# Where the sequence additions, the check's sums and the next norm stand in an adaLN, Fourier mixing and SwiGLU block

## The chip, the cores and the metric

The kernel runs on one core of one Trainium2 chip. The metric is the device time of one execution in microseconds (us); the time before is a median of 710.24 us. TensorE (PE) does the matrix products, VectorE (DVE) and ScalarE (ACT) work on tiles of 128 partitions, GpSimd (POOL) and SyncE (SP) mostly start transfers.

## The reference

`x` has 2048 rows of 512 columns. Six vectors of 512 come from `silu(c) @ w_mod`; they shift, scale and gate the two halves of the block.

```python
mod = (_silu(c) @ w_mod).reshape(c.shape[0], 6, 1, -1)
sa, ca, ga, sb, cb, gb = (mod[:, 0], ..., mod[:, 5])
h = _layernorm(x, axis=-1) * (1 + ca) + sa
# y = Real(DFT_seq(DFT_hidden(h))):  a = h @ Wd_re.T, b = h @ Wd_im.T,  y = Ws_re @ a - Ws_im @ b
x = x + ga * _A_ref(h, A_dft_seq_re, A_dft_seq_im, A_dft_hid_re, A_dft_hid_im)
h = _layernorm(x, axis=-1) * (1 + cb) + sb
# out = (silu(h @ w1) * (h @ w3)) @ w2, with 1792 inner columns
x = x + gb * _B_ref(h, B_w1, B_w3, B_w2)
```

## The kernel before, in words

Every fp32 product is made of three products of parts (`product`, L100): high by high, high by low, low by high. ACT makes a high part (a copy in the short format, L87), DVE the low part (the rest, L90). So each tile that PE is to multiply passes through ACT and then DVE.

The work has three stages. First come the first norm and the transform over the 512 columns, ordered by a small planner (`task`, `arrange`). Then comes the transform over the 2048 rows ("the sequence stage", `seq_unit`, L750): 32 units in two halves `j`, and while PE runs a unit, DVE prepares a later one (tiles `l`, `d`, `bh`). At last comes the feed-forward part. The output has four groups of 512 rows, `t` = 0 to 3, in two pairs `PAIRS = ((0, 2), (1, 3))`. Groups 0 and 2 are ready after the first half of the sequence stage, 1 and 3 after the second.

The order inside each engine is the order in which the Python code records instructions. Work that has no fixed place waits in a queue `background` of steps, each with an estimate of its DVE and ACT time. After each piece of PE work `advance` takes steps from the queue until the time of that piece is used up; a `PAUSE` ends one such turn. A second queue, `jobs`, holds the splitting of weights and goes first.

The names that the prediction uses:

- `mod_columns` makes one of four vectors (`ga`, `sb`, `cb1`, `gb`) on DVE: weights `wmc` times `silu(c)` (step `scale`, L96), then sums (step `total`, L356 and L362).
- `residual` (L805) adds a gated result to a group's rows `xr`. `add_sums` does it twice for a group, from a copy `sum` of accumulators; after the second half of the sequence stage four such steps, eight instructions, stand at the end of `background`.
- `ln2(t)` is the second norm of group `t` as some 25 steps: `a1` to `a3` the mean and the difference `xc`, `a3b` squares on ACT, `a4`, `rows` and `partition_sums` the sum of squares, `a6` the root on ACT (with a table load), `a6b` its inverse and spread over rows, `a7` the product (DVE, L96) and `a8` scale and shift (ACT, L894). Between them are `PAUSE`s. `chunk_parts` then splits `xc` into `h2h` (ACT) and `h2l` (DVE), the right-hand operand of `up`.
- `up(g, t)` runs four `up_block`s of 12 matmuls, `w1` then `w3` for two halves `q`. A `w1` block ends in a Silu on ACT (L1094), a `w3` block in a product `v` on DVE (L96), a high part `hf` on ACT and its low part on DVE. `up` uses PSUM banks 0 to 3 in turn.
- `down_unit` is six matmuls with `w2`; here it uses banks 4 to 7 in turn, and ACT empties each (`y`, L335). POOL starts the transfer that adds two of them to the result in memory (L1146).
- After `up(0, 0)` and `up(1, 0)` come eight `down` units of group 0, called D1 to D8 here, then `up(0, 2)`, which needs `h2h` and `h2l` of group 2. D5 takes the bank that D1 used.
- From then on 12 `items` run in seven "factor" units for `w1` (`a1` to `a7`) and seven for `w3` (`b1` to `b7`), with eight `down` units (`y`) between. `turning` is 5, the first item of pair 1. The last factors of an item run in the head of the next: `-b7 a1 a2 -b4 -b3`. `b4` adds to the bank that DVE must have read after `b7`.
- `judge` adds up sums of squares (`chk`) which tell whether the matrices have the symmetry that the kernel uses: a memset of `sq` on POOL (L1005) and 14 small DVE instructions (L1006 to L1026).

Of the kernel before, what the change touches and what calls it, by code (L numbers as in the profile page):

```python
# [8 lines left out]
F32 = mybir.dt.float32  # L9
# [3 lines left out]
OP = mybir.AluOpType  # L13
AX = mybir.AxisListType

P = 128
N = 512
# [5 lines left out]
ND = D // P  # L23
# [19 lines left out]
def folded(nc, pools, c, cp, wmr, wmc, x, xt, ctr, cti, wdr, wdi, w1, w3, w2, out):  # L43
# [8 lines left out]
    consts, small, big, psum, dram, tc = pools  # L52
# [6 lines left out]
    def take(dt=F32, what="s"):  # L59
        slot = free.popleft()  # L60
        count[0] += 1
        t = big.tile([P, 2, N], dt, name=f"{what}_{count[0]}", tag=f"slot{slot}")
        slot_of[id(t)] = (slot, t)
        return t

    def give(t):
        slot, _ = slot_of.pop(id(t))
        free.append(slot)

    def bank(i):  # L70
# [12 lines left out]
    def cols(i):  # L83
        return slice(i * P, (i + 1) * P)

    def copy(dst, src, scale=1.0):
        nc.scalar.activation(dst, src, AF.Copy, scale=scale)  # L87
# [7 lines left out]
    def times(dst, a, b):  # L95
        nc.vector.tensor_tensor(out=dst, in0=a, in1=b, op=OP.mult)  # L96

    def product(acc, lhs, rhs, first, last, more=False):
        for n, (a, b) in enumerate(PASSES):
            nc.tensor.matmul(  # L100
                acc,
                lhs[a],
                rhs[b],
                start=first and n == 0,
                stop=last and n == len(PASSES) - 1,
                skip_group_check=more,
            )


    background = deque()  # L110
# [3 lines left out]
    def step(queue, slots, fn, dve=0.0, act=0.0):  # L114
        queue.append((slots, dve, act, fn))
# [128 lines left out]
    for k in range(2, 4):  # L244
# [7 lines left out]
        out=ident,  # L252
        in_=ident,
# [9 lines left out]
        out=anti,  # L263
        in_=anti,
# [72 lines left out]
    sc_row = []  # L337
# [6 lines left out]
    def mod_columns(v, dst):  # L344
        w = {}

        def fetch(i):
            w[i] = take(F32, "wmc")
            nc.sync.dma_start(w[i], wmc[v, i])

        def scale(i):
            times(w[i], w[i], sc_row[0][:, 0, :].unsqueeze(1).to_broadcast([P, 2, N]))

        def total(i):
            r1 = small.tile([P, 32], F32, name=f"r1_{v}_{i}", tag="r1")
            nc.vector.tensor_reduce(  # L356
                out=r1,
                in_=flat(w[i]).rearrange("p (a b) -> p a b", b=32),
                axis=AX.X,
                op=OP.add,  # L360
            )
            nc.vector.tensor_reduce(  # L362
                out=dst[:, 2 * i : 2 * i + 2],
                in_=r1.rearrange("p (a b) -> p a b", b=16),
                axis=AX.X,
                op=OP.add,
            )
            give(w[i])

        def end():  # L370
            if dst is cb1:
                nc.vector.tensor_scalar(cb1, cb1, 1.0, None, op0=OP.add)
            if dst is ga:
                nc.vector.tensor_scalar(ga2, ga, -2.0, None, op0=OP.mult)
            if dst is gb:
                give(sc_row[0])
            done.add(("mod", v))

        for i in range(2):
            step(background, 1, lambda i=i: fetch(i))  # L380
        background.extend([PAUSE] * 2)
        for i in range(2):
            step(background, 0, lambda i=i: scale(i), 1.2)
            step(background, 0, lambda i=i: total(i), 1.3)
        step(background, 0, end, 0.1)


# [427 lines left out]
    xc, sums = {}, {}  # L815
# [187 lines left out]
    def judge():  # L1003
        sq = consts.tile([P, 3, 32], F32, name="sq")
        nc.gpsimd.memset(sq, 0.0)  # L1005
        nc.vector.tensor_reduce(  # L1006
            out=sq[:, 0, :8],
            in_=chk.rearrange("p a b n -> p (a b) n"),
            axis=AX.X,
            op=OP.add,  # L1010
        )
# [12 lines left out]
        times(fine[:, 0:2], fine[:, 0:2], fine[:, 2:4])  # L1024
        times(fine[:, 0:1], fine[:, 0:1], fine[:, 1:2])
        nc.vector.tensor_scalar(bad, fine[:, 0:1], -1.0, 1.0, op0=OP.mult, op1=OP.add)  # L1026
# [25 lines left out]
    def give_w(key):  # L1052
        for t in wuse.pop(key):
            give(t)

    hf = {}
    turn = [0, 0]
    cur = {}
# [4 lines left out]
    def behind(units, fn):  # L1063
        if units:
            later.setdefault(units, []).append(fn)
        else:
            fn()
# [5 lines left out]
            later[n - 1] = later.pop(n)  # L1073


    def up_block(g, t, q, w):
        if q == 0 and w == "w1":
            drain(lambda: ("h2", t, 1) in done)
        to = bank(turn[0] % 4)
        turn[0] += 1  # L1080
        for d in range(ND):
            at = slice(d * P, (d + 1) * P)
            product(
                to,
                [u[:, q, at] for u in wuse[w, g]],
                [u[t, d // 2][:, d % 2, :] for u in (h2h, h2l)],
                d == 0,
                d == ND - 1,
            )
        if t == PAIRS[0][1] and q == 1:  # L1090
            give_w((w, g))
        if w == "w1":
            cur["v"] = take(F32, "v")
            nc.scalar.activation(cur["v"][:, 0, :], to, AF.Silu)  # L1094
        else:
            v = cur.pop("v")
            times(v[:, 1, :], v[:, 0, :], to)
            u = hf[g, t, q] = take(F32R, "hf")
            copy(u[:, 0, :], v[:, 1, :])
            behind(1, lambda: minus(u[:, 1, :], v[:, 1, :], u[:, 0, :].bitcast(F32)))  # L1100
            behind(1, lambda: give(v))
# [395 lines left out]
    for m in range(2):  # L1497
        todo.popleft()
        name = f"seq{m}"
# [53 lines left out]
                w_low((w, 0))  # L1553
    give(zz)

    USED = {"w1": (0.0, 0.5), "w3": (1.2, 0.5), "y": (0.0, 0.6), "own": (0.7, 0.0)}
    FACTOR = {
# [6 lines left out]
    def beside(us, used):  # L1566
        advance(us - used[0], us - used[1], jobs)
        if not jobs:
            advance(0.0, 0.0)

    def up(g, t):
        for q in range(2):
            for w in ("w1", "w3"):
                drain(lambda: ((w, g), "l") in done, jobs)
                delayed()
                up_block(g, t, q, w)
                beside(2.72, USED[w])

    def down(g, pair, t, d, key):
        drain(lambda: (key, "l") in done, jobs)  # L1580
# [13 lines left out]
    for g in range(2):  # L1594
        for d in range(ND):
            down(g, 0, 0, d, ("w2", g))
    judge()
    up(0, 2)
    load_w(("w3", *items[0]))
    weight_jobs(0, "w1")  # L1600
# [8 lines left out]
    turning = len([at for at in items if at[1] == 0])  # L1609
# [45 lines left out]
        beside(1.36, FACTOR[kind][n])  # L1655

    weight_jobs(0, "w3")
    ln2(1)
    ln2(3)
    for i in range(len(items)):  # L1660
        body = "a6 a5 y a7 y y a4 y a3 y b1 y b2 y b6 b5 y"
        if i == turning:
            body = "y y y y y a6 y a5 y a7 y b1 b2 a4 b6 a3 b5"
        if i == len(items) - 1:
            body = "a6 a5 y a7 y y a4 y a3 b1 y b2 b6 b5 y b7 y b4 y b3 y y y y y y y y"
        head = "-b7 a1 -b4 -b3 a2 " if i == turning else "-b7 a1 a2 -b4 -b3 " if i else "a1 a2 "
# [813 lines left out]
```

## Time and profile before

| | |
|---|---|
| time, median of 3 runs | 710.24 us (709.85 to 710.78) |
| the profiled execution's own time | 708.46 us |
| its span in the profile | 706.7 us |
| mean granted PE clock | 0.991 |
| PE busy | 686.3 us, 97% |
| DVE busy | 548.3 us, 78% |
| ACT busy | 430.8 us, 61% |
| POOL busy | 119.4 us, 17% |

The profile is of one execution. Its times count from the start of the span. A timeline row reads: start, duration, engine, source line, operation, output tile, input tiles, shape, how many, and in brackets how long the engine stood idle before it and which instruction ended that.

### The profile page before, as it was taken

Reading aid. Unit: us, or ns where it says so; the run is one execution under the profiler, and the core shown is the slowest. Engines: PE = TensorE matmul, PEld = TensorE weight load, DVE = VectorE, ACT = ScalarE, POOL = GpSimd, SP = SyncE. Lnnn points to the kernel's source line nnn. Section 1 sums busy time; section 2 is a strip of 40 time slices with the busy share of each in tenths; the row PEclk is TensorE's granted clock in tenths of the full one; section 3 lists DMA queues with packets and bytes.
Section 4 is the critical chain, followed back from the end, with each engine's and each line's share of the span. In section 5 each row is a group of like instructions: output and inputs, shape, how many; then the busy total and the mean of one; then the engine's idle time right before and its main releaser. Section 6 shows DMA issues by size and latency. Waiting matters only on the chain.

```text
span 706.7 us, 8912 instructions
## 1 busy us (share of the span) xinstructions
PE 686.3 (97%) x3152; PEld 564.7 (80%) x3152; DVE 548.3 (78%) x877; ACT 430.8 (61%) x709; POOL 119.4 (17%) x141
## 2 busy tenths in 40 slices
PE   7999999999999999899999999999999999999995
PEld 4898888888888888687888788787788888888784
DVE  5999679997999978579987886896865556664763
ACT  4998865545454655745677676867665565656420
POOL 1320253542524000200100101011010100101000
PEclk9999999999999999999999999999999999999998
DMA  8730299796678521522868558376763847537403
GB/s 266 211 120 1 77 373 328 251 307 229 207 283 287 168 86 41 92 58 64 209 114 199 89 130 153 61 156 137 239 136 73 180 62 175 111 69 162 137 0 124
DMA packets 38100, 108.93 MB, mean 154 GB/s; under 512 B 4896, under 2 KB 5152, under 8 KB 38048
## 3 DMA queue, kind: packets, MB, share of 16 engines
q0 software_dynamic: 12352, 43.00, 29.3%
q1 hardware_dynamic: 25264, 63.98, 27.5%
q10 hardware_dynamic: 432, 1.31, 0.5%
q8 instruction: 26, 0.43, 0.3%
q14 instruction: 26, 0.21, 0.1%
HBM read 76.81 MB, written 33.55 MB: 156 GB/s over the span
## 4 chain that ended last, share of the span: by engine, by line
PE 81%; DVE 7%; ACT 6%; issue 2%; DMA 2%; SPq 1%; ACTq 0%; DVEq 0%
PE bank L100 52%; PE bank L750 25%; PE bank L559 2%; PE bank L598 1%; DMA wmr<-in_wmr 1%; ACT xc L894 1%; PE bank L576 1%; DVE xc L96 1%; SPq L231 1%; ACT hf L87 1%; ACT y L335 1%; DVE v L96 0%; DVE hl L90 0%; ACT hm L501 0%; DMA w<-in_wdi 0%
## 5 line engine op out<-in xcount | busy, mean ns | idle before, releaser
L100 PE MATMUL bank<-hf,w2h 128*128 128x512 f32 (+1 forms) x452 | 140.9, 391 | 0.3
L1146 POOL DMA_DIRECT2D sum<-y x48 | 41.0, 855 | 390.1 <-ACT y L335 373.0
L100 PEld LDWEIGHTS bank<-hf,w2h 128*128 128x128 f32 x452 | 84.3, 188 | 22.1 <-DVE hf L90 3.4
L100 PE MATMUL bank<-hf,w2l 128*128 128x512 f32 (+1 forms) x226 | 87.6, 388 | 0.0
L87 ACT ACTIVATE hf<-v 128x512 fp32r<-128x512 f32 x56 | 35.3, 630 | 67.3 <-DVE v L96 62.7
L335 ACT ACTIVATE y<-bank,gb 128x512 f32<-128x512 f32 x96 | 64.9, 682 | 18.6 <-PE bank L100 18.3
L93 DVE TENSOR_TENSOR v<-bank,x 128x512 f32<-128x512 f32 x36 | 24.7, 685 | 34.9 <-PE bank L100 34.8
L750 PE MATMUL bank<-bh,us 128*128 128x512 f32 x128 | 49.9, 390 | 0.0
L93 DVE TENSOR_TENSOR x<-bank,x 128x512 f32<-128x512 f32 x36 | 24.7, 687 | 32.4 <-PE bank L100 28.7
L750 PE MATMUL bank<-bh,ul 128*128 128x512 f32 x128 | 49.8, 389 | 0.0
L750 PE MATMUL bank<-d,us 128*128 128x512 f32 x128 | 49.8, 389 | 0.0
L750 PE MATMUL bank<-d,uh 128*128 128x512 f32 x128 | 49.8, 389 | 0.0
L750 PE MATMUL bank<-l,us 128*128 128x512 f32 x128 | 49.8, 389 | 0.0
L750 PE MATMUL bank<-l,uh 128*128 128x512 f32 x128 | 49.8, 389 | 0.0
L100 PEld LDWEIGHTS bank<-hf,w2l 128*128 128x128 f32 x226 | 42.4, 188 | 8.4
L90 DVE TENSOR_TENSOR hf<-v,hf 128x512 fp32r<-128x512 f32 x56 | 38.5, 687 | 12.2 <-ACT hf L87 12.1
L170 POOL DMA_INDIRECT re<-in_ctr,mirror x32 | 35.8, 1117 | 66.2 <-DVE ul L90 39.5
L1224 ACT ACTIVATE v<-v 128x512 f32<-128x512 f32 x36 | 22.8, 632 | 38.8 <-DVE v L93 38.8
L87 ACT ACTIVATE x<-bank 128x512 f32<-128x512 f32 x72 | 41.4, 586 | 7.2 <-PE bank L100 6.5
L170 POOL DMA_INDIRECT im<-in_cti,mirror x32 | 32.7, 1023 | 35.3 <-PE bank L750 10.0
L100 PE MATMUL bank<-h2h,w1h 128*128 128x512 f32 x80 | 31.8, 397 | 1.5 <-ACT h2h L87 1.5
L100 PE MATMUL bank<-h2l,w1h 128*128 128x512 f32 x80 | 31.9, 399 | 0.8 <-DVE h2l L90 0.8
(246 smaller groups left out, 1775.2 us busy)
## 6 DMA issues: line engine op xcount, KB each, us to landing
sum<-y POOLq DMA_DIRECT2D x48, 512.0 KB, 5.6
w<-in_w SPq DMA_DIRECT2D x42, 512.0 KB, 4.5
re<-in_ctr SPq DMA_DIRECT2D x32, 256.0 KB, 5.0
im<-in_cti SPq DMA_DIRECT2D x32, 256.0 KB, 5.0
wmc<-in_wmc SPq DMA_DIRECT2D x8, 512.0 KB, 6.3
xr<-in_xt SPq DMA_DIRECT2D x8, 512.0 KB, 7.6
sum<-xr SPq DMA_DIRECT2D x8, 512.0 KB, 6.2
x<-in_x SPq DMA_DIRECT2D x11, 256.0 KB, 4.8
```

The lines of the kernel that those rows point to most:

```text
L87: nc.scalar.activation(dst, src, AF.Copy, scale=scale)
L90: nc.vector.tensor_tensor(out=dst, in0=a, in1=b, op=OP.subtract)
L93: nc.vector.tensor_tensor(out=dst, in0=a, in1=b, op=OP.add)
L96: nc.vector.tensor_tensor(out=dst, in0=a, in1=b, op=OP.mult)
L100: nc.tensor.matmul(acc, lhs[a], rhs[b], start=first and n == 0, stop=last and n == len(PASSES) - 1, skip_group_check=more,)
L170: nc.gpsimd.indirect_dma_start(dst, None, rows, bass.IndirectOffsetOnAxis(ap=at, axis=0))
L231: queue.dma_start(raw_w[dt][q * 64 : (q + 1) * 64, m, :], w[i][par::2, q])
L335: nc.scalar.activation(dst, src, AF.Identity, scale=by)
L559: nc.tensor.matmul(halves(hb[k])[:, m, :], sides((hh, hl)[a][k])[:, dt, m, :], wu[dt][:, b, m, :], start=False, stop=dt % 2 == 1 and n == ...
L750: nc.tensor.matmul(acc[what, e], lhs, rhs, start=begin and i == 0, stop=(end or (turn and what == "x")) and i == len(terms) - 1, skip_grou ...
L1146: nc.gpsimd.dma_start(sums[t, d // 2], y, accum_op=OP.add)
L1224: behind(k != 0 or q == 0, lambda: nc.scalar.activation(v, src, AF.Silu))
```

## The change

It does five things. `mod_columns` uses, in place of one product over 1024 columns and one sum of it, eight multiply-and-sum instructions of 128 columns (with `accum_out`), and each step has an estimate of 0.9 us where two had 1.2 and 1.3. `fill_pauses`, called once after the sequence stage, takes the six last steps of `background` (the four `add_sums` and two releases of tiles) and puts each `add_sums` ahead of one of the last four pauses of `ln2(2)`. `up_block` is recorded in two halves, with a turn of `advance` after each. `ln2(1)` and `ln2(3)` enter the queue ahead of `up(0, 2)`. `judge` moves from there to the head of item 7.

```diff
-            step(background, 0, lambda i=i: scale(i), 1.2)
-            step(background, 0, lambda i=i: total(i), 1.3)
+            for b in range(2):
+                step(background, 0, lambda i=i, b=b: total(i, b), 0.9)
...
+        def total(i, b):
+            sums, junk = parts[i], w[i][:, b, :]
+            for n in range(ND):
+                nc.vector.scalar_tensor_tensor(
+                    junk[:, cols(n)], junk[:, cols(n)], 1.0, sc_row[0][:, 0, cols(n)],
+                    op0=OP.mult, op1=OP.mult, accum_out=sums[:, b, n : n + 1],
+                )
...
+    def fill_pauses():
+        last = [background.pop() for _ in range(6)][::-1]
+        fillers = [last[:1], last[1:3], last[3:4], last[4:]]
+        at = len(background)
+        while fillers:
+            at -= 1
+            if background[at][-1] is None:
+                for slots, _, _, fn in fillers.pop()[::-1]:
+                    background.insert(at, (slots, 0.0, 0.0, fn))
...
-                up_block(g, t, q, w)
-                beside(2.72, USED[w])
+                for part in range(2):
+                    up_block(g, t, q, w, part)
+                    beside(1.36, USED[w] if part else (0.0, 0.0))
...
-    judge()
+    ln2(1)
+    ln2(3)
     up(0, 2)
...
     weight_jobs(0, "w3")
-    ln2(1)
-    ln2(3)
     for i in range(len(items)):
+        if i == turning + 2:
+            judge()
```

In the listings below a row is line, operation, output, inputs and shape; numbers after a name count tiles.

ACT from the last high part of `up(1, 0)` through the first `down` units, before. `v_2714` is the last product of `up(1, 0)`, `y_2743` and `y_2769` empty the banks of D1 to D4, `xc_2564` and `xc_2611` are the two halves of group 2 in `a8`:

```order
L87 ACTIVATE hf_2737<-v_2714 128x512
L880 ACT_TABLE_LOAD
L880 ACTIVATE s_377_2721<-s_377_2721,eps 32x16
L335 ACTIVATE y_2743<-bank_382_2744,gb 128x512
L335 ACTIVATE y_2743<-bank_383_2759,gb 128x512
L335 ACTIVATE y_2769<-bank_385_2770,gb 128x512
L894 ACTIVATE xc_2564<-xc_2564,sb,cb_151 128x512 x2
L335 ACTIVATE y_2769<-bank_386_2780,gb 128x512
```

and now, from the root of `ln2(2)` on; `v_2781` is the last product, `hf_2805` its high part, `y_2812` empties D1 and D2, `xc_2546` and `xc_2616` are the halves of group 2:

```order
L883 ACT_TABLE_LOAD
L883 ACTIVATE s_364_2700<-s_364_2700,eps 32x16
L1101 ACT_TABLE_LOAD
L1101 ACTIVATE v_2734<-bank_368_2721 128x512
L87 ACTIVATE w2h_2736<-w_366_2716 128x1024
L87 ACTIVATE w2h_2747<-w_367_2718 128x1024
L87 ACTIVATE hf_2765<-v_2734 128x512
L1101 ACTIVATE v_2781<-bank_376_2768 128x512
L897 ACTIVATE xc_2546<-xc_2546,sb,cb_151 128x512 x2
L87 ACTIVATE hf_2805<-v_2781 128x512
L897 ACTIVATE xc_2616<-xc_2616,sb,cb_151 128x512 x2
L335 ACTIVATE y_2812<-bank_382_2813,gb 128x512
```

The root and its two table loads now stand ahead of the splitting of `w2`, and both halves of `a8` and the last `hf` ahead of the first `y`.

DVE over the same stretch, before: the last product of `up(1, 0)`, the inverse root, `a7` twice and the low parts of group 2.

```order
L96 TENSOR_TENSOR v_2714<-v_2714,bank_378_2723 128x512
L90 TENSOR_TENSOR hf_2737<-v_2714,hf_2737 128x512
L883 RECIPROCAL s_377_2721<-s_377_2721 32x16
L847 COPY w_382_2753<-s_377_2721 32x16 x4
L848 STREAM_TRANSPOSE stat_2556<-w_382_2753 128x512
L96 TENSOR_TENSOR xc_2564<-xc_2564,stat_2556 128x1024
L96 TENSOR_TENSOR xc_2611<-xc_2611,stat_2556 128x1024
L90 TENSOR_TENSOR h2l_2821<-xc_2564,h2h_2819 128x1024
```

and now:

```order
L90 TENSOR_TENSOR w2l_2749<-w_367_2718,w2h_2747 128x1024
L886 RECIPROCAL s_364_2700<-s_364_2700 32x16
L850 COPY w_374_2752<-s_364_2700 32x16 x4
L851 STREAM_TRANSPOSE stat_2538<-w_374_2752 128x512
L96 TENSOR_TENSOR v_2734<-v_2734,bank_372_2740 128x512
L90 TENSOR_TENSOR hf_2765<-v_2734,hf_2765 128x512
L96 TENSOR_TENSOR xc_2546<-xc_2546,stat_2538 128x1024
L808 SCALAR_TENSOR_TENSOR xr_2382<-sum_2605,ga,xr_2382 128x512 x2
L96 TENSOR_TENSOR xc_2616<-xc_2616,stat_2538 128x1024
L808 SCALAR_TENSOR_TENSOR xr_2106<-sum_2605,ga,xr_2106 128x512 x2
L96 TENSOR_TENSOR v_2781<-v_2781,bank_378_2786 128x512
L90 TENSOR_TENSOR hf_2805<-v_2781,hf_2805 128x512
```

The inverse, both `a7` and four of the eight additions (`xr`) now stand ahead of the last product `v_2781`, which stood ahead of them; the other four additions stand further up, two on either side of the second product of `up(0, 0)`.

POOL around the memset of `judge`, before, with the transfers that start after D4, D6 and D8 ahead of it:

```order
L1146 DMA sum_1_2265<-y_2769 128x1024
L1146 DMA sum_0_2263<-y_2790 128x1024
L1146 DMA sum_1_2265<-y_2810 128x1024
L1005 MEMSET sq 128x96
L1146 DMA sum_0_2631<-y_3074 128x1024
```

There it stood behind the last transfer of D1 to D8. POOL now:

```order
L1153 DMA sum_1_3155<-y_4704 128x1024
L1153 DMA sum_0_3591<-y_4746 128x1024
L1153 DMA sum_1_3593<-y_4794 128x1024
L1008 MEMSET sq 128x96
L1153 DMA sum_0_3153<-y_4934 128x1024
```

The memset stands behind the start of a `down` result's transfer in both; now that is the last `down` unit of item 6, directly ahead of `b7`. On DVE the 14 instructions stand between the last work for that `down` unit and the addition that reads the bank of `b7`.

More of the change, by code (lines that the diff above doesn't have):

```diff
@@ L349, in fetch @@
             nc.sync.dma_start(w[i], wmc[v, i])
[L351 to L368, printed above, removed]
+        def total(i, b):
+            sums, junk = parts[i], w[i][:, b, :]
+            for n in range(ND):
+                nc.vector.scalar_tensor_tensor(
+                    junk[:, cols(n)],
+                    junk[:, cols(n)],
+                    1.0,
+                    sc_row[0][:, 0, cols(n)],
+                    op0=OP.mult,
+                    op1=OP.mult,
+                    accum_out=sums[:, b, n : n + 1],
+                )
+            if b:
+                nc.vector.tensor_reduce(
+                    out=dst[:, 2 * i : 2 * i + 2], in_=sums, axis=AX.X, op=OP.add
+                )
+                give(w[i])
+        parts = [
+            small.tile([P, 2, ND], F32, name=f"r1_{v}_{i}", tag="r1") for i in range(2)
+        ]
         def end():
@@ L1073, in delayed, with up_block @@
             later[n - 1] = later.pop(n)
-    def up_block(g, t, q, w):
-        if q == 0 and w == "w1":
+    def up_block(g, t, q, w, part):
+        if q == 0 and w == "w1" and part == 0:
             drain(lambda: ("h2", t, 1) in done)
-        to = bank(turn[0] % 4)
-        turn[0] += 1
-        for d in range(ND):
+        if part == 0:
+            cur["to"] = bank(turn[0] % 4)
+            turn[0] += 1
+        to = cur["to"]
+        for d in range(2 * part, 2 * part + 2):
             at = slice(d * P, (d + 1) * P)
@@ L1089, in up_block @@
             )
+        if part == 0:
+            return
         if t == PAIRS[0][1] and q == 1:
@@ L1554, in folded @@
     give(zz)
+    def fill_pauses():
[7 more added lines that the diff above has]
+                    background.insert(at, (slots, 0.0, 0.0, fn))
+    fill_pauses()
     USED = {"w1": (0.0, 0.5), "w3": (1.2, 0.5), "y": (0.0, 0.6), "own": (0.7, 0.0)}
```

## The prediction

> **What bounds the kernel now.** I read the page's busy shares first, then the chain of work that ended last in order of time.
>
> ```profile
> PE 686.3 (97%) x3152; PEld 564.7 (80%) x3152; DVE 548.3 (78%) x877; ACT 430.8 (61%) x709; POOL 119.4 (17%) x141
> PE 81%; DVE 7%; ACT 6%; issue 2%; DMA 2%; SPq 1%; ACTq 0%; DVEq 0%
> ```
>
> ```profile
> 88.22 174.32 PE bank L750 x768
> ...
> 262.54 21.77 PE bank L100 x96
> ...
> 297.97 23.21 PE bank L100 x95
> ```
>
> PE is busy for 97% of the span and fills 81% of the chain, so an edit to DVE or ACT counts only where PE waits. In the sequence stage PE runs 768 matmuls in 174.32 us, 0.227 us each, with no other piece between: nothing waits there. One `up_block` of 12 is 2.72 us, one `down` unit of 6 is 1.36 us. The largest hole lies between 262.54 and 297.97, where `up(0, 2)` has to start. PE's timeline and the stretches with their granted clock (the number ahead of the DMA share) show it:
>
> ```profile
> 284.14 0.62 PE L100 MATMUL bank<-hf,w2h 128*128 128x512 f32 x2
> ...
> 289.58 0.62 PE L100 MATMUL bank<-hf,w2h 128*128 128x512 f32 x2
> ...
> 294.80 0.39 PE L100 MATMUL bank<-hf,w2l 128*128 128x512 f32 x1
> 296.71 0.51 PE L100 MATMUL bank<-h2h,w1h 128*128 128x512 f32 x1 [1.53 <-ACT h2h L87]
> 297.97 0.79 PE L100 MATMUL bank<-h2l,w1h 128*128 128x512 f32 x1 [0.76 <-DVE h2l L90]
> ```
>
> ```profile
> 297.50:300.90 3.40, 2.93 (x7) 2.35 (x8) 2.72 (x7) 1.96 (x2) 1.03 (x2) 0.50 1.10 176
> ```
>
> D1 starts at 284.14, D5 at 289.58. The first matmul of `up(0, 2)` could start at 294.80 + 0.23 = 295.03 and starts at 296.71, waiting for `h2h`: 1.68 us. The second could start at 296.94 and starts at 297.97, waiting for `h2l`: 1.03. Then the clock is halved until 300.90, which costs (300.90 - 297.97)/2 = 1.47. Together 4.2 us. That is what an earlier second norm can win here. The later holes are each under 1 us (the one at 389.32 below is of this kind).
>
> **The eight additions and the earlier root: `up(1, 0)` and D1 to D8.** The rows for the sum, DVE and then ACT:
>
> ```profile
> 261.22 2.73 DVE L805 SCALAR_TENSOR_TENSOR xr<-bank,ga,xr 128x512 f32<-128x512 f32 x4 [1.17 <-PE bank L750]
> ...
> 277.76 2.36 DVE L90 TENSOR_TENSOR w2l<-w,w2h 128x1024 fp32r<-128x1024 f32 x2 [1.80 <-ACT w2h L87]
> ...
> 280.63 0.69 DVE L93 TENSOR_TENSOR t<-t 128x512 f32<-128x512 f32 x1
> ...
> 282.70 0.68 DVE L90 TENSOR_TENSOR hf<-v,hf 128x512 fp32r<-128x512 f32 x1
> ...
> 284.02 0.25 DVE L840 TENSOR_REDUCE s<-q 32x16 f32<-32x64 f32 x1
> ...
> 287.42 0.24 DVE L883 RECIPROCAL s<-s 32x16 f32<-32x16 f32 x1 [0.93 <-ACT s L880]
> ...
> 289.18 2.36 DVE L96 TENSOR_TENSOR xc<-xc,stat 128x1024 f32<-128x1024 f32 x2
> ...
> 329.09 2.73 DVE L805 SCALAR_TENSOR_TENSOR xr<-sum,ga,xr 128x512 f32<-128x512 f32 x4
> ```
>
> ```profile
> 260.77 0.60 ACT L87 ACTIVATE sum<-bank 128x512 f32<-128x512 f32 x1 [0.31 <-PE bank L750]
> ...
> 276.68 2.00 ACT L87 ACTIVATE w2h<-w 128x1024 fp32r<-128x1024 f32 x2
> ...
> 285.13 0.63 ACT L87 ACTIVATE hf<-v 128x512 fp32r<-128x512 f32 x1 [2.91 <-DVE v L96]
> 285.78 1.28 ACT L880 ACT_TABLE_LOAD   x1
> 287.08 0.31 ACT L880 ACTIVATE s<-s,eps 32x16 f32<-32x16 f32 x1
> 287.29 1.82 ACT L335 ACTIVATE y<-bank,gb 128x512 f32<-128x512 f32 x3
> 290.49 1.53 ACT L894 ACTIVATE xc<-xc,sb,cb 128x512 f32<-128x512 f32 x2 [1.37 <-issue]
> ```
>
> These give: a 128x1024 DVE step 1.18, two additions 1.36, a `v` or `hf` step on DVE 0.6, the fold of squares to its sum (280.63 to 284.27, less the 0.6 of `hf`) 3.0, the inverse and its spread (287.42 to 289.18) 1.76; on ACT `hf` 0.63, one split of `w2` 1.0, a table load 1.28, the root 0.31, a `y` 0.6, both parts of one `a8` 1.53.
>
> I follow the new order on the times of before. Until the four additions from banks end (261.22 + 2.73 = 263.95) nothing has been late. ACT is free of the copies `sum` at 261.37; two squares and two splits of weights (taken at 1.0 each, as the splits of `w2`), a table load and a Silu (0.6) last until 267.2. DVE: `a3` of the second half, `w1l`, `w3l` and `a4` are four steps of 1.18, to 268.6; `v` 269.2; a wait for `hf` on ACT, then its low part, 270.6; the fold, 273.6; two additions, 275.0; the second `v` (its block ended at 284.14 - 4 x 2.72 = 273.3), 275.6; two additions and a low part, 277.5. ACT meanwhile does `hf` (276.3), load, root, load (279.1), the Silu that has been ready since 276 (279.7) and only then `w2h`, 280.7. DVE waits 3.2 us for that, then two `w2l` 283.0, the inverse 284.8, `v` 285.4, the wait for `hf` and the low part 286.7, `a7` 287.9, two additions 289.2, `a7` 290.4, two additions 291.7, and the last product `v` at 292.3 (in the order before, its `hf` could start at 285.13). ACT follows with `hf` (293.0), the second `a8` (294.5) and the first `y`, 295.1. That `y` empties the bank that D5 needs. D5 could start at 289.6 and starts at about 295.1: PE idles 5.5 us. `h2h` and `h2l` of group 2 then come while D5 to D8 run, so the old hole of 4.2 us is gone.
>
> Who waits: behind the late `v` on DVE stand only `hf` and `h2l`; behind the late `y` on ACT stand `h2h` and the next `y`, and behind D5 everything on PE. Bounds for the idle time: DVE waits for ACT 4.6 us in all on the way; with half of that saved, 3.1 us; with an `a8` pair more of delay, 7.0.
>
> The clock. The clock was halved once more in this trace, for 3.4 us behind a stretch of 3.4 us in which PE was busy for 1.60:
>
> ```profile
> 68.80:72.20 3.40, 1.60 (x9) 1.03 (x8) 3.40 (x6) 3.40 (x8) 0.00 (x0) 1.00 0.00 0
> 72.20:75.60 3.40, 3.40 (x18) 3.40 (x18) 2.86 (x4) 2.28 (x5) 0.00 (x0) 0.50 0.00 0
> ```
>
> A hole of 5.5 us empties such a stretch wherever it begins. The halved time after PE resumes depends on where in the stretch that is: 1.7 to 5.1 us, so 0.85 to 2.6 lost; I take half of 3.4, 1.7. Sum for this place: 5.5 + 1.7 - 4.2 = 3.0 us slower (3.1 + 0.85 - 4.2 = -0.2 to 7.0 + 2.6 - 4.2 = 5.4).
>
> One rule speaks of the loads. The table load row lasts 1.28 us, and the root starts 1.30 us after the load did. The Trainium skill ("ScalarE: Activation LUTs", What ACT_TABLE_LOAD costs) gives 1283 ns for the load, which agrees, and a drain of about 1380 ns on top of it, of which this row shows nothing. By that rule the two loads ahead of `w2h` would add an estimated 2.8 us to the hole.
>
> **Judge's sums at item 7.** The rows from its old place and from the head of item 7:
>
> ```profile
> 298.63 0.84 POOL L1146 DMA_DIRECT2D sum<-y  x1 [2.35 <-ACT h2h L87]
> 299.17 0.50 POOL L1005 MEMSET sq<- 128x96 f32 x1
> ...
> 533.15 0.85 POOL L1146 DMA_DIRECT2D sum<-y  x1 [5.95 <-ACT y L335]
> ```
>
> ```profile
> 299.70 0.42 DVE L1006 TENSOR_REDUCE sq<-chk 128x8 f32<-128x256 f32 x1 [0.27 <-POOL sq L1005]
> ...
> 302.66 0.14 DVE L1026 TENSOR_SCALAR bad<-fine 1x1 int32<-1x1 f32 x1
> ...
> 533.60 0.69 DVE L93 TENSOR_TENSOR x<-bank,x 128x512 f32<-128x512 f32 x1 [3.64 <-PE bank L100]
> ```
>
> ```profile
> 536.05 0.39 PE L100 MATMUL bank<-th,w3h 128*128 128x512 f32 x1
> ```
>
> The 14 instructions take 302.80 - 299.70 = 3.1 us. At the old place they stood beside PE's halved clock and delayed no matmul. At the new place the memset stands on POOL behind the transfer of the last `down` unit, which starts at 533.15; it can start 0.54 us after that and end at 534.2. DVE then does the sums until 537.3, and only then the addition that reads the bank of `b7`, until 538.0. `b4` (the matmul at 536.05) needs that bank: 2.0 us of waiting. Bounds: 1.5 if the transfer and the memset overlap more, 2.4 if a low part for the next `down` unit is late too. Whether the clock is halved after it is open: the quoted stretch with 1.8 us idle was followed by half clock, and a hole of 2.0 us falls into one stretch with 1.8 of it in about half the cases. That would cost 1.7 more. I take 2.0, range 1.5 to 4.1.
>
> **The multiply-and-sum steps.**
>
> ```profile
> L96 DVE TENSOR_TENSOR wmc<-wmc,scr 128x1024 f32<-128x1024 f32 x8 | 9.8, 1222 | 0.0
> L356 DVE TENSOR_REDUCE r<-wmc 128x32 f32<-128x1024 f32 x8 | 9.8, 1220 | 0.3
> L401 DVE SCALAR_TENSOR_TENSOR wu<-w,wu 128x256 fp32r<-128x256 f32 x4 | 1.7, 417 | 0.0
> ```
>
> ```profile
> 100.00:262.00 162.00, 162.00 (x716) 134.00 (x715) 147.19 (x207) 85.78 (x166) 52.23 (x52) 1.00 0.73 247
> ```
>
> Before, 16 instructions take 19.6 us; now there are 64. From 256 columns at 0.417 and 512 at 0.68 (2.73/4) a plain one of 128 is some 0.27 us; reading the sum out is in no row. Bounds 0.27 to 0.6 each, so 17 to 38 us; I take 0.4, 26 us. DVE has 14.8 us free between 100 and 262, so 6 us more fits, and 19 would not quite. I count nothing.
>
> **The rest.** Halving `up_block` and queueing `ln2(1)` and `ln2(3)` sooner puts these norms one item earlier; their `a8` steps stand at the same units of an item, so I expect the small holes to move, not go. One is
>
> ```profile
> 389.32 0.50 PE L100 MATMUL bank<-th,w1sh 128*128 128x512 f32 x1 [0.49 <-ACT x L87]
> ```
>
> I count 0, bounds -0.8 and 0.8.
>
> **Sum.** 3.0 + 2.0 = 5.0 us. The profiled execution took 708.46 us and would take 713.5; the median of the runs is 710.24, and on it the time is 715.2.
>
> **Rivals.**
>
> *The norm's gain is real.* If the last `v` ends by 289.6 - 0.63 - 1.53 - 0.6 = 286.8 (ACT does the root and `w2h` in gaps that I have put too late), D1's bank is empty when D5 wants it, and the 4.2 us are won. With the sums' 2.0: 708.0. For it: the norm itself does come sooner. Against: DVE's own work between 263.95 and that `v`, without any wait, is 292.3 - 263.95 - 4.6 = 23.8 us, which ends at 287.7. Chance 0.09. That the sums hide as well, as the change has it, gives 706.0: 0.03.
>
> *Only D5 waits:* the sums find a gap. 713.2, chance 0.09. Against: nothing lies between the memset and DVE's wait.
>
> *The multiply-and-sum steps outrun the sequence stage.* At 0.6 each DVE lacks 19 - 14.8 = 4 us there, and `seq_unit`s wait: 719.2. Chance 0.07.
>
> *The drain* of the rule above: 5.0 + 2.8, 718.0. Chance 0.04, since the load's row shows none.
>
> **How the numbers follow.** The forecast has the remaining 0.68, and its own range is -0.2 + 1.5 to 5.4 + 4.1, 711.5 to 719.7, with the ends unlikely together. The range 711.4 to 719.2 holds it nearly whole and two rivals; the faster cases (0.12) and the worst ends stay out. A difference of 0.2%, 1.4 us, is about what a measurement can tell from none. Faster 0.12, same 0.05 (the low end of the forecast), slower 0.83.
>
> **What would show it.** Right: a PE wait of 4 to 7 us ahead of the fifth `down` unit, released by ACT's `y`, and half clock after it; no wait of the first `up(0, 2)` matmul for `h2h`; a wait of about 2 us at item 7's `b4`, released by DVE's `x`. DVE's last product of `up(1, 0)` ends near 292. Wrong: D5 follows D4 at once, or PE waits in the sequence stage, or the multiply-and-sum rows last over 0.6 us.

## The result, and the profile after

The changed kernel takes 718.6 us (median of 4 runs, 717.4 to 720.0) where the kernel before took 710.05 on the same chip: a ratio of 1.0126 with an interval of 1.0107 to 1.0146. That is 8.55 us slower. The forecast was 715.2 with a range up to 719.2. The profiled execution took 720.0 us, its span is 718.1.

The chain of work that ended last, from the page of the changed kernel:

```profile
PE 70%; DVE 14%; ACT 8%; issue 3%; DMA 2%; SPq 1%; another core or an unknown queue 1%; POOL 0%; ACTq 0%
```

PE fell from 81% to 70% of the chain, and DVE rose from 7% to 14%: somewhere PE now waits for long pieces of DVE work. The three longest waits of PE in the feed-forward part of the changed kernel say where. They are at D5, at the first item's `a6` and at item 7's `b4`; in brackets stand the wait and what ended it:

```profile
297.74 1.22 PE L100 MATMUL bank<-hf,w2h 128*128 128x512 f32 x2 [5.09 <-ACT y L335]
331.64 0.50 PE L100 MATMUL bank<-th,w1sh 128*128 128x512 f32 x1 [1.94 <-ACT x L87]
547.18 0.50 PE L100 MATMUL bank<-th,w3h 128*128 128x512 f32 x1 [1.80 <-DVE x L93]
```

The first and the third were forecast, the second was not. The neighbourhood of the first two by stretch, with the granted clock (the number ahead of the DMA share):

```profile
291.29:294.70 3.41, 1.36 (x7) 0.79 (x5) 3.41 (x6) 0.99 (x2) 0.00 (x0) 1.00 0.49 126
294.70:298.11 3.41, 0.37 (x1) 0.37 (x2) 1.04 (x2) 3.03 (x5) 0.00 (x0) 0.50 0.07 30
298.11:301.53 3.42, 3.42 (x9) 2.65 (x9) 1.99 (x2) 3.42 (x6) 0.99 (x1) 0.50 0.47 47
328.84:332.25 3.41, 1.47 (x7) 0.89 (x6) 2.68 (x7) 2.72 (x4) 0.00 (x0) 1.00 0.06 25
332.25:335.66 3.41, 3.41 (x10) 2.63 (x9) 1.83 (x3) 2.46 (x4) 0.00 (x0) 0.50 0.23 29
```

The wait of D5 is followed by half clock until 301.53 (PE works in 297.74 to 301.53, so 1.9 us are lost), that of `a6` by half clock from 332.25 to 335.66 (1.7 us lost).

**Where the time went.** PE runs the same matmuls in the same order in all these kernels. The table gives, for every kernel run here, how much later (+) or sooner (-) than in the kernel before a matmul starts, at five places of the program. It counts from the start of the sequence stage, behind the addition `ho` of the last section. It is worked out from the matmuls' start times in the profiled executions; "ratio" is that of the timed runs. One execution is not the median: the column "end" differs from what the ratio gives by up to 1.7 us (e3: +4.5, and 2.8 by the ratio).

| kernel | in `up(0, 2)` | after first `a6` | in item 4 | after `b4` of item 7 | end | ratio (interval) |
|---|---|---|---|---|---|---|
| changed | +2.9 | +6.2 | +6.4 | +8.4 | +8.5 | 1.0126 (1.0107, 1.0146) |
| e1_judge_back | +3.3 | +10.2 | +10.4 | +10.4 | +10.4 | 1.0133 (1.0112, 1.0154) |
| e2_norm_back | +3.4 | +2.8 | +0.4 | +2.5 | +2.6 | 1.0032 (1.0019, 1.0045) |
| e3_additions_last | -2.8 | +3.8 | +0.7 | +4.5 | +4.5 | 1.0040 (1.0021, 1.0059) |
| e4_whole_blocks | -2.7 | -3.2 | -6.3 | -4.3 | -4.2 | 0.9933 (0.9913, 0.9953) |
| e5_sums_only | -3.2 | -1.7 | -0.7 | -0.6 | -0.5 | 0.9999 (0.9984, 1.0014) |
| e6_halves_only | -1.9 | +2.1 | -0.3 | -0.3 | -0.3 | 1.0007 (0.9993, 1.0020) |
| e7_whole_judge_back | -2.5 | +0.7 | -2.4 | -2.5 | -2.4 | 0.9957 (0.9943, 0.9972) |
| e8_whole_judge_spread | -2.6 | -3.2 | -6.3 | -6.3 | -6.5 | 0.9929 (0.9915, 0.9944) |
| e9_spread_norm_back | -2.7 | -3.3 | -5.6 | -5.6 | -5.9 | 0.9911 (0.9896, 0.9925) |
| e10_spread_additions_last | -4.2 | -4.8 | -3.8 | -3.8 | -4.0 | 0.9953 (0.9940, 0.9965) |
| e11_spread_again | -2.7 | -3.3 | -6.3 | -6.4 | -6.6 | 0.9914 (0.9901, 0.9927) |
| e12_whole_again | -2.7 | -3.2 | -6.3 | -4.1 | -4.0 | 0.9946 (0.9933, 0.9960) |

The changed kernel's row is the result in one line: +2.9 in `up(0, 2)`, that is from D5, +3.3 at the first `a6`, +0.2 over items 1 to 4, +2.0 at `b4`, +0.1 after it. Together 8.5, and 8.55 were measured. The two are closer than one execution each can promise. The spans of the two profiled executions differ by 11.4 us: 1.2 us of that arise ahead of the sequence stage, where the other kernels with the same `mod_columns` lie between -0.9 and +0.5, and 1.7 at its start, ahead of the table's zero (last section).

**D5.** ACT and DVE rows of the changed kernel, to be held against those before:

```profile
279.08 1.28 ACT L883 ACT_TABLE_LOAD   x1
280.37 0.31 ACT L883 ACTIVATE s<-s,eps 32x16 f32<-32x16 f32 x1
280.70 1.28 ACT L1101 ACT_TABLE_LOAD   x1
281.99 0.60 ACT L1101 ACTIVATE v<-bank 128x512 f32<-128x512 f32 x1
282.49 2.00 ACT L87 ACTIVATE w2h<-w 128x1024 fp32r<-128x1024 f32 x2
...
295.08 0.63 ACT L87 ACTIVATE hf<-v 128x512 fp32r<-128x512 f32 x1 [2.80 <-DVE v L96]
295.61 1.50 ACT L897 ACTIVATE xc<-xc,sb,cb 128x512 f32<-128x512 f32 x2
297.02 1.24 ACT L335 ACTIVATE y<-bank,gb 128x512 f32<-128x512 f32 x2
```

```profile
293.04 1.41 DVE L808 SCALAR_TENSOR_TENSOR xr<-sum,ga,xr 128x512 f32<-128x512 f32 x2
294.37 0.68 DVE L96 TENSOR_TENSOR v<-v,bank 128x512 f32<-128x512 f32 x1
```

This is the forecast chain: root and two table loads ahead of `w2h`, additions ahead of the last product (294.37; this trace enters the sequence stage 2.9 us later than the one before, so 291.5 on the times before, forecast 291.7), then `hf`, an `a8` pair and the first `y`.

**The first `a6`.** Before, DVE waited for PE's bank ahead of the last product of `up(1, 2)`, and PE waited 0.23 us at `a6`:

```profile
321.28 0.69 DVE L96 TENSOR_TENSOR v<-v,bank 128x512 f32<-128x512 f32 x1 [0.81 <-PE bank L100]
324.11 0.50 PE L100 MATMUL bank<-th,w1sh 128*128 128x512 f32 x1 [0.23 <-ACT x L87]
```

DVE and ACT of the changed kernel ahead of it:

```profile
324.99 0.69 DVE L841 COPY q<-r 32x16 f32<-32x16 f32 x4
...
327.67 1.23 DVE L90 TENSOR_TENSOR xc<-xr,stat 128x1024 f32<-128x1024 f32 x1
328.82 0.68 DVE L96 TENSOR_TENSOR v<-v,bank 128x512 f32<-128x512 f32 x1
```

```profile
329.53 0.63 ACT L87 ACTIVATE hf<-v 128x512 fp32r<-128x512 f32 x1 [4.58 <-DVE v L96]
330.07 1.04 ACT L875 ACTIVATE sq<-xc 128x1024 f32<-128x1024 f32 x1
331.01 0.58 ACT L87 ACTIVATE x<-bank 128x512 f32<-128x512 f32 x1
```

Steps of `ln2(1)`, from the sums over partitions to `xc` (324.99 to 328.82: 3.8 us without a pause), now stand ahead of the last product of `up(1, 2)`. ACT waits 4.58 us for that product, then does its `hf`, a square of `ln2(1)` (1.04 us), and only then the copy `x` that empties the bank which `a6` needs.

**The check's sums.** POOL and DVE of the changed kernel at item 7, with the first instruction of the sums and the addition behind them (there are 15 instructions, not the 14 counted ahead of the result; the 3.1 us stand):

```profile
542.32 0.85 POOL L1153 DMA_DIRECT2D sum<-y  x1 [5.95 <-ACT y L335]
542.86 0.50 POOL L1008 MEMSET sq<- 128x96 f32 x1
```

```profile
543.39 0.42 DVE L1009 TENSOR_REDUCE sq<-chk 128x8 f32<-128x256 f32 x1 [4.27 <-POOL sq L1008]
...
546.43 0.69 DVE L93 TENSOR_TENSOR x<-bank,x 128x512 f32<-128x512 f32 x1
```

The memset stands behind the transfer, as forecast. DVE had stood idle for 4.27 us until it, then did 3.1 us of sums, and `b4` waited for the addition.

**Multiply-and-sum.** The line in the changed kernel (count, then busy time in us and the mean of one in ns):

```profile
L354 DVE SCALAR_TENSOR_TENSOR wmc<-wmc,scr 128x128 f32<-128x128 f32 x64 | 14.5, 286 | 0.0
```

### The profile page after: what moved, and what is told of

It is laid out like the page before. It is cut to its first block, busy times and chain, and to the rows that moved or that the text cites. A ratio compares the mean times of both kernels' runs of the same rounds, so it can differ in the third digit from the quotient of the medians.

```text
span 718.1 us, 9030 instructions
## 1 busy us (share of the span) xinstructions
PE 689.5 (96%) x3152; PEld 565.3 (79%) x3152; DVE 543.3 (76%) x989; ACT 431.2 (60%) x709; POOL 122.9 (17%) x141
## 4 chain that ended last, share of the span: by engine, by line
PE 70%; DVE 14%; ACT 8%; issue 3%; DMA 2%; SPq 1%; another core or an unknown queue 1%; POOL 0%; ACTq 0%
PE bank L100 44%; PE bank L753 24%; DVE v L96 2%; DMA wmr<-in_wmr 1%; PE bank L562 1%; ACT hf L87 1%; DVE xc L96 1%; PE bank L601 1%; DVE xr L808 1%; ACT y L335 1%; SPq L231 1%; DVE xc L90 1%; ACT xc L897 1%; DVE ul L90 1%
## 5 line engine op out<-in xcount | busy, mean ns | idle before, releaser
L100 PE MATMUL bank<-hf,w2h 128*128 128x512 f32 (+1 forms) x452 | 142.6, 395 | 5.4 <-ACT y L335 5.1
L170 POOL DMA_INDIRECT re<-in_ctr,mirror x32 | 34.0, 1063 | 69.3 <-DVE ul L90 38.5
L170 POOL DMA_INDIRECT im<-in_cti,mirror x32 | 38.1, 1189 | 30.4 <-issue 11.9
L100 PE MATMUL bank<-th,w1sh 128*128 128x512 f32 x72 | 29.1, 405 | 2.9 <-ACT x L87 2.9
L100 PE MATMUL bank<-h2h,w1l 128*128 128x512 f32 x80 | 31.2, 390 | 0.2 <-DVE w1l L90 0.2
```

The lines of the kernel that those rows point to most:

```text
L100: nc.tensor.matmul(acc, lhs[a], rhs[b], start=first and n == 0, stop=last and n == len(PASSES) - 1, skip_group_check=more,)
L170: nc.gpsimd.indirect_dma_start(dst, None, rows, bass.IndirectOffsetOnAxis(ap=at, axis=0))
```

## The experiments

Each is the changed kernel, or the one before, with one thing different. A first set takes the parts of the change back one at a time.

**e1_judge_back**: the check's sums back at their old place.

```diff
+    judge()
     ln2(1)
     ln2(3)
     up(0, 2)
...
-        if i == turning + 2:
-            judge()
```

> The changed kernel (1.0126 of before) with the check's sums back ahead of up(0, 2). Theory: the wait of item 7's b4 (a step of 2.18 us) goes back to the usual 0.2, and the sums cost nothing at the old place: 2.2 us less, 716.4 us, ratio 1.0095. Rival: at the old place the 3.1 us of DVE now delay h2l of group 2 or the next norm, and the time stays within 0.5 us of 718.6.

Measured: 720.14 us, ratio 1.0133, no gain. The wait of `b4` is gone, as both said. But the wait of the first `a6` grew:

```profile
332.34 0.80 PE L100 MATMUL bank<-th,w1sh 128*128 128x512 f32 x1 [4.78 <-ACT x L87]
```

```profile
306.09 0.42 DVE L1009 TENSOR_REDUCE sq<-chk 128x8 f32<-128x256 f32 x1 [0.64 <-POOL sq L1008]
...
309.12 3.47 DVE L90 TENSOR_TENSOR tl<-xc,th 128x1024 fp32r<-128x1024 f32 x3
```

The sums stand in the middle of DVE's work for group 2 (`tl`). From there to `a6` DVE has next to no slack, so their 3.1 us arrive at `a6` nearly whole: 4.78 - 1.94 = 2.8. The half clock lasts from 330.56 to 337.39, 3.4 us longer than in the changed kernel; PE works in 5.1 us of it, so 2.5 are lost there, not 1.7. That makes 3.6 at `a6`, and 0.4 were lost in `up(0, 2)` (second column of the table: +10.2 against +6.2). The theory was wrong on the sum and right on `b4`. The rival had the time right by the ratio (0.0007 apart, 0.5 us), but not the place.

**e2_norm_back**: `ln2(1)` and `ln2(3)` behind the weight jobs of item 0.

```diff
-    ln2(1)
-    ln2(3)
     up(0, 2)
...
     weight_jobs(0, "w3")
+    ln2(1)
+    ln2(3)
```

> The changed kernel with ln2(1) and ln2(3) queued behind the weight jobs of item 0 again. Theory: the missed loss of 3.2 us at the first a6 (a step of 2.33 us and 3.4 us of half clock behind it) comes from the fold and the spread of ln2(1) that stand on DVE ahead of the last product of up(1, 2): the step falls to about 0.5 and the half clock behind it goes, 715.4 us, ratio 1.0080. Rival: the halved up blocks alone make that product late; the step stays over 1.5 us and the time over 717.5.

Measured: 713.0 us, ratio 1.0032. The row of the first `a6` has no bracket, so PE did not wait:

```profile
328.80 0.39 PE L100 MATMUL bank<-th,w1sh 128*128 128x512 f32 x1
```

With the blocks halved, the sooner norm is shown to cause that wait. The gain is larger than expected (the table: +8.5 to +2.6, 5.9 us), since the small holes of items 1 to 4 go as well: +2.8 falls to +0.4, where the changed kernel stays at +6.2 to +6.4.

**e3_additions_last**: `fill_pauses()` not called.

```diff
-    fill_pauses()
```

> The changed kernel with the four steps of sequence additions left at the end of the queue. Theory: the additions hold DVE in the chain to the last product of up(1, 0) (1.3 us ahead of the second product, 2.6 us ahead of the last): the first y comes some 3.8 us sooner, the wait of D5 falls from 5.1 to 1.3 us, and the half clock behind it may go: 712.9 to 714.8 us, ratio about 1.0050. Rival: the order on ACT alone (root and two table loads ahead of the splits of w2, a8 ahead of the first y) sets the wait: it stays over 4 us and the time over 717.5.

Measured: 713.58 us, ratio 1.0040. D5:

```profile
292.04 0.73 PE L100 MATMUL bank<-hf,w2h 128*128 128x512 f32 x2 [1.18 <-ACT y L335]
```

The wait falls from 5.09 to 1.18, forecast 1.3, and no half clock follows. With the blocks halved, the additions are shown to make 3.9 us of that wait. But the first `a6` now waits longer (the wait below), with 6.8 us of half clock from 325.30 on, in which PE works from 326.53. DVE has two of the additions ahead of the third product of `up(1, 2)` and steps of `ln2(1)` ahead of the last; which of the two makes this wait was not run apart.

```profile
PE bank L100 <- ACT x L87: 4.3, 1, 4.3
```

**e4_whole_blocks**: each `up_block` followed by one turn of the queue.

```diff
                 for part in range(2):
                     up_block(g, t, q, w, part)
-                    beside(1.36, USED[w] if part else (0.0, 0.0))
+                beside(2.72, USED[w])
```

> The changed kernel with each up block recorded whole, with one turn of the queue behind it. The root then stands behind the splits of w2 and the first y ahead of both a8, while the additions stay early. Theory: the last product ends near 290.7 and the first y near 291.9, so D5 waits under 0.7 us; the first matmul of up(0, 2) waits 0.5 to 2 us again; the missed loss at the first a6 stays: 712 to 714 us, ratio about 1.0040. Rival: the additions alone make D5 wait, over 3 us, and the time stays over 716.

Measured: 705.75 us, ratio 0.9933, faster than the kernel before and better than the 712 to 714 expected. ACT:

```profile
278.13 2.00 ACT L87 ACTIVATE w2h<-w 128x1024 fp32r<-128x1024 f32 x2
...
285.07 1.28 ACT L883 ACT_TABLE_LOAD   x1
...
289.34 0.63 ACT L87 ACTIVATE hf<-v 128x512 fp32r<-128x512 f32 x1 [0.75 <-DVE v L96]
289.88 0.67 ACT L335 ACTIVATE y<-bank,gb 128x512 f32<-128x512 f32 x1
```

`w2h` is again ahead of the root, and the first `y` ahead of both `a8`. It is 7.1 us sooner than in the changed kernel, of which 1.4 are this trace's earlier sequence stage. D5 does not wait. What the expectation missed is that the first `a6` does not wait either, although the norm is queued as soon as in the changed kernel: with one turn for each block the fold of `ln2(1)` is not yet in front of the last product. Against the changed kernel the table shows 5.6 us won at D5, 3.9 at `a6` and 3.2 in items 1 to 4. The wait of `b4` stays.

A second set: e5 to e8 on another chip, e9 to e12 on one more.

**e5_sums_only**: the kernel before with the new `mod_columns`.

> The kernel before with the multiply-and-sum steps alone. Theory: they are hidden, the sequence stage stays at 174.3 us and the time at 710.2 (709.5 to 711). Rival: the late start of DVE's ho ahead of the sequence stage (1.9 us late, PE waiting 0.5 to 1.5 us for it), which all five traces of the changed kernel and its variants show and the one of before does not, comes from these steps and the sooner fetches of wmc: then it shows here as well, and the time is 711.2 to 711.8.

Measured: 707.34 us beside 707.92 for the kernel before, ratio 0.9999: no difference. The late `ho` of the rival isn't there (last section). But the trace is not that of the kernel before. ACT, and PE at the start of `up(0, 2)`:

```profile
282.89 1.28 ACT L883 ACT_TABLE_LOAD   x1
...
287.15 0.63 ACT L87 ACTIVATE hf<-v 128x512 fp32r<-128x512 f32 x1 [0.75 <-DVE v L96]
```

```profile
295.62 0.39 PE L100 MATMUL bank<-h2h,w1h 128*128 128x512 f32 x1
```

The root's table load now stands ahead of the last `hf`, not behind it, and `up(0, 2)` waits for nothing: the hole of 4.2 us is gone. The edit of `mod_columns` alone does that. The queue's estimate for its steps is 16 x 0.9 = 14.4 us, where the old ones had 8 x (1.2 + 1.3) = 20, so the queue behind them runs ahead. Most of the 4.2 us come back in three places: 1.0 us around a wait of 0.8 us for DVE's `xr` at 132 us, 1.5 us by the first `a6`, 1.0 in items 1 to 4.

The first of these is not the edit's. DVE's order up to there is the same in every kernel with the new `mod_columns`, and e7 and e8 on the same chip lose only 0.1 to 0.2 us there. In e5 and e6 the transfer of `c` landed later, ACT and then DVE started later behind it, and `xr` was late. ACT in e5, then in e7 (counted from the same matmul at the stage's start, 0.9 us sooner):

```profile
101.39 0.63 ACT L342 ACTIVATE scr<-scr 128x512 f32<-128x512 f32 x1 [3.39 <-DMA scr<-in_c]
```

```profile
100.95 0.63 ACT L342 ACTIVATE scr<-scr 128x512 f32<-128x512 f32 x1 [2.52 <-DMA scr<-in_c]
```

**e6_halves_only**: the kernel before with the new `mod_columns` and the halved blocks.

> The kernel before with the multiply-and-sum steps and the halved up blocks, and nothing moved: additions last, check's sums and ln2(1), ln2(3) at their old places. Theory: halving alone brings the root ahead of the splits of w2 and makes D5 wait (a step of about 1.6 us, as without the additions), in return the first up(0, 2) matmuls no longer wait, and the first a6 does not wait over 0.5: 707.5 to 710 us. Rival: halving alone makes the first a6 late too (step over 1.5 us with half clock): over 712.

Measured: 708.02 us, ratio 1.0007: no difference. The table's first column is 1.3 us behind that of e5. PE's waits:

```profile
PE bank L100 <- DVE v L96: 2.0, 1, 2.0
PE bank L100 <- ACT y L335: 1.6, 2, 1.2
PE bank L100 <- ACT x L87: 1.5, 1, 1.5
```

D5 waits 1.2 us, as the theory had it, and the first `up(0, 2)` matmuls don't. But 4.0 us are lost by the first `a6` (-1.9 to +2.1): a matmul just ahead of it waits 2.0 for a product `v` of `up(1, 2)`, which now stands behind two additions, and `a6` 1.5. Theory and rival each had a half of it.

**e7_whole_judge_back**: e4 with the sums ahead of `up(0, 2)`, the edit of e1.

> The changed kernel with whole up blocks (705.75 us, ratio 0.9933) and the check's sums back ahead of up(0, 2). Theory: DVE has over 3 us of slack there when the blocks are whole, since neither up(0, 2) nor the first a6 waits long for it: the wait of b4 (2.0 us) goes and nothing comes: 703.7 us, ratio 0.9905. Rival: the sums are paid at the first a6 or at h2l of group 2, as with the halved blocks: 705.5 to 708.

Measured: 704.68 us, ratio 0.9957. The rival: `b4` no longer waits, `a6` does.

```profile
323.25 0.50 PE L100 MATMUL bank<-th,w1sh 128*128 128x512 f32 x1 [1.89 <-ACT x L87]
```

With the half clock that follows, 3.9 us are lost there (+0.7 against -3.2), where `b4` costs 2.1. The sums hold DVE for more than their 3.1 us: it first stands idle for POOL's memset, which it did for only 0.64 us in e1.

```profile
304.21 0.42 DVE L1009 TENSOR_REDUCE sq<-chk 128x8 f32<-128x256 f32 x1 [2.44 <-POOL sq L1008]
```

**e8_whole_judge_spread**: e4 with the sums as four steps in the queue, entered at item 7.

```diff
+        for fn in (first, second, third, fourth):
+            step(background, 0, fn, 0.8)
+            background.append(PAUSE)
```

> The changed kernel with whole up blocks and the check's sums as four steps of 0.8 us in the queue, entered at item 7 where the sums stood in one piece. Theory: only the length of the piece made b4 wait; in four pieces behind b4's own additions they hide in DVE's pauses, 2.0 us less than 705.75: 703.7 us, ratio 0.9905. Rival: item 7 has no DVE time to spare and each piece delays a unit by part of its 0.8 us: 705 to 708.

Measured: 702.34 us, ratio 0.9929. `b4` does not wait. The ratio could not be told from that of e4 on the other chip (0.9933), so both were run again side by side, with two more.

**e11_spread_again**, **e12_whole_again**:

> The kernel with whole up blocks and the check's sums in four steps once more, beside three others on one chip: ratio 0.9929 as before, and 1.8 to 2.0 us less than the kernel with whole blocks and the sums in one piece.

> The changed kernel with whole up blocks once more, on the same chip as the one with the sums in four steps. Theory: b4 costs it 1.8 to 2.0 us (the step of 2.18 us in its trace), ratio 0.9955. Rival: the wait is made up later, and both take the same time within 0.5 us, as their ratios on two chips (0.9933 and 0.9929) would have it.

Measured: 703.64 us (0.9914, 0.9901 to 0.9927) and 706.42 us (0.9946, 0.9933 to 0.9960). The intervals do not meet: the sums in one piece cost 2 to 3 us, the step of `b4` in the trace 2.0. DVE in e11 shows how the pieces hide, the first of the 15 instructions behind the addition that `b4` needs:

```profile
528.31 0.69 DVE L93 TENSOR_TENSOR x<-bank,x 128x512 f32<-128x512 f32 x1 [3.65 <-PE bank L100]
...
529.65 0.41 DVE L1014 TENSOR_REDUCE sq<-chk 128x8 f32<-128x256 f32 x1
```

Cutting the sums into pieces and putting them behind that addition came together here; one without the other was not run.

**e9_spread_norm_back**: e8 with the edit of e2.

> Whole up blocks, sums in four steps, but ln2(1) and ln2(3) queued behind the weight jobs of item 0 as in the kernel before. Theory: the moved additions give the gain, since they no longer stand in the first items; the norm's place is worth nothing with whole blocks: ratio within 0.001 of the one with the norm sooner (0.993). Rival: the sooner norm is what clears the small holes of the first items (some 1.3 us each): 2 us or more slower than with it, ratio 0.996 or more.

Measured: 704.37 us, ratio 0.9911 beside 0.9914. With whole blocks the norm's place is worth nothing that can be measured.

**e10_spread_additions_last**: e8 without `fill_pauses()`.

> Whole up blocks, sums in four steps, the norm sooner, but the sequence additions at the end of the queue. Theory: the 5.4 us of additions stand again in up(0, 2) and the first item, ahead of the first a6, and that step rises over 1.5 us, the up(0, 2) hole is back to 1 us or more: 3 us or more slower than with them moved, ratio 0.997 or more. Rival: with whole blocks the additions hide at either place: ratio 0.993.

Measured: 706.9 us, ratio 0.9953 (0.9940 to 0.9965): about 3 us slower than e11, as expected, but not for the reason given. In the table this kernel is ahead of e11 up to the first `a6` (-4.8 against -3.3) and behind it in item 4 (-3.8 against -6.3). So the moved additions cost 1.5 us around D5 and win 4.1 in the small holes of items 1 to 4, which stay in e10:

```profile
PE bank L100 <- ACT x L87: 1.0, 2, 0.5
```

The fastest version is e8 (run twice: 0.9929 and 0.9914) or e9: the change without its halving, and with the sums spread.

## Why the prediction was right, and where it was not

*The sum.* 5.0 us were forecast and 8.55 measured. The two terms of the sum, D5 and the check's sums, are there at their price (+2.9 and +2.0); the rest, most of it at the first `a6`, was not foreseen. The time lies in the range, 0.6 us under its end, and that is in part luck: the room was there for a longer wait of D5, half clock behind `b4` and two rivals, none of which happened.

*D5.* Right in chain, place and size: 5.1 us of wait, 5.5 forecast; 1.9 us of half clock, 1.7 forecast; +2.9 for the place, +3.0 forecast. The runs make the reason sharper. With the new `mod_columns` and the sooner norm in all four (the check's sums come only later, at item 7), the first column has -4.2 with neither halves nor early additions (e10), -2.7 with the additions alone (e11), -2.8 with the halves alone (e3), and +2.9 with both. Each alone costs some 1.5 us there, both together 7.1: either leaves ACT and DVE enough room ahead of D5, the two do not. And the old hole goes by the new estimates in `mod_columns` (e5), which the prediction had costed for their time only, not as what orders the queue; since it read the new order itself, its sum did not suffer.

*The rest.* This term is the one that failed: 0 with bounds of 0.8, and +3.5 was there, 3.3 of it at the first `a6`. The step said that the norms' `a8` steps stand at the same units of an item, one item earlier, so the small holes would move and not go. That part held (items 1 to 4: +0.2). It looked only at the items. The first steps of `ln2(1)`, fold, mean and `xc`, had moved into `up(1, 2)`, ahead of a product that ACT and PE wait for, and they were not costed against it. e2 and e4 show that in the changed kernel it takes both the sooner norm and the halved blocks. They are not the only way to lose that place: in e6, with halved blocks, the norm back and the additions last, 4.0 us are lost by there.

*The check's sums.* +2.0 forecast, +2.0 found, no half clock behind it. The prediction called the old place free because no matmul was late there. e1 and e7 show that in the new order it is not: 3.9 to 4.0 us, twice the price of item 7.

*Multiply-and-sum.* Hidden, as counted: the changed kernel leaves the sequence stage at 0.0 of the table, and e5 takes as long as the kernel before. The size was off to the safe side: 0.29 us each, not 0.4. As each starts ahead of the end of the one before it, the 64 keep DVE busy for 14.5 us, not 26, and less than the 19.6 of the old instructions.

*The drain.* Rows first: the root starts 1.29 us after its table load, the Silu 1.29 us after the second load (279.08, 280.37; 280.70, 281.99). The Trainium skill ("ScalarE: Activation LUTs", What ACT_TABLE_LOAD costs) would have about 1.38 us more behind each; the trace does not agree, and that rival falls.

*The rivals with a gain* fell with D5. The gain that they counted on, 4.2 us at `up(0, 2)`, is there in full in e5 and e10.

## What to carry to other kernels

When a change gives a queue more turns, everything behind those turns comes sooner, also what nobody meant to move: list, for each engine, what now stands ahead of the next product that the matmul engine waits for. A changed estimate is such a change as well. Two edits that each gain at a place can lose there together, so run them one at a time. A piece of 3 us that nobody waits for costs up to its length, and half clock on top, where the engine has no slack up to the next hand-over (2.0 us at `b4`, 3.9 to 4.0 by the first `a6`); in pieces of 0.8 us behind the hand-over it cost nothing here.

## What the runs showed of the hardware

*The clock.* Half clock came and went in stretches of 3.41 us at fixed distances (291.29, 294.70, 298.11, and 328.84 is 11 such stretches after 291.29). Of all such stretches at full clock between 20 and 690 us in the 14 traces, eight had PE busy for 0.36 to 1.60 us, and half clock followed each. Nine had 1.66 to 2.02, and it followed none. Of ten with 1.61 or 1.62 it followed eight. `b4` is such a case: not in the changed kernel,

```profile
543.90:547.31 3.41, 1.61 (x8) 1.04 (x7) 2.99 (x16) 0.00 (x0) 0.00 (x0) 1.00 1.02 179
```

but in e3:

```profile
536.95:540.36 3.41, 1.62 (x7) 1.03 (x7) 3.03 (x15) 0.00 (x0) 0.00 (x0) 1.00 0.93 129
540.36:543.77 3.41, 3.41 (x9) 2.62 (x9) 2.07 (x4) 2.33 (x5) 0.00 (x0) 0.50 0.13 25
```

So a wait of about 1.9 us costs 1.7 more when all of it falls into one stretch (3.4 - 1.9 leaves 1.5 busy), and nothing more when it is split so that over 1.66 stay busy in each. The Trainium skill ("TensorE: Matmul & The Clock Gate", What's actually happening) gives a free-running window of 3413 ns, which agrees. Its later rule (HAM oscillation), "no PE-idle gaps >~3.4µs", does not agree with these traces: half clock followed the waits of 1.94 us here and of 1.89 us in e7.

*A late start.* In the trace of the changed kernel and in all eight of two chips (e1 to e4, e9 to e12) DVE's `ho`, at the start of the sequence stage, starts after 3.5 to 4.4 us of idle time, released by something that the trace can't name, and PE waits 0.7 to 1.6 us for it. In the four of a third chip (e5 to e8) and in the profile of before, the idle time is 1.7 and the releaser PE's bank. It is not the edit: e8 and e11 are one and the same kernel, and e11 has the late start. The changed kernel, then e7:

```profile
91.92 0.69 DVE L93 TENSOR_TENSOR ho<-bank,ho 128x512 f32<-128x512 f32 x1 [4.19 <-remote]
```

```profile
88.25 0.69 DVE L93 TENSOR_TENSOR ho<-bank,ho 128x512 f32<-128x512 f32 x1 [1.73 <-PE bank L579]
```

On those chips the kernel before took 710.05 to 710.23 us, on the third chip 707.92; the profile of before (708.46 us) has no late `ho`. That the late start makes this difference fits in size, but was not tested, and its cause stays open. Ratios taken on one chip are free of it, and so is the table, which counts from behind that place.
